# Two attention blocks on one core: the last twenty rounds with exponentials of 1024 columns, and the last head folded into the last group's projection

## The chip, the cores and the metric

The kernel runs on one core of a Trainium2 chip. The metric is the device time of one execution, in microseconds: 2844.2 us is the median of three runs (2843.77 to 2844.33).

## The reference

Two multi-head attention blocks A and B read the same x (2048 tokens, 512 features, 32 heads of 16), and a gate mixes their results:

```python
x = A_x
g = _sigmoid((x * gate_w).sum(-1, keepdims=True))
a = _A_ref(x, A_wqkv, A_wo)      # qkv = x @ wqkv; softmax(q k^T / 4) v per head; @ wo
b = _B_ref(x, B_wqkv, B_wo)
return g * a + (1 - g) * b
```

## The kernel before

After a prologue (the projections q, k, v) the kernel goes through 64 heads, 32 of block A and 32 of block B. A head has 16 tiles of 128 keys, and a **round** is one head and one tile of keys: 1024 rounds in all (`ROUNDS`). In a round, TensorE makes four score products of 128 keys by 512 queries (`score`, L594; product L602), ScalarE takes the exponential of each from PSUM (L604), and TensorE multiplies the exponentials with the values (`attend`, L555; product L563) into one PSUM bank `acc`. It has four column groups of 32 rows, one for each quarter of the queries; row 16 of a group is the sum of the exponentials, the softmax's denominator.

The scores carry the row's maximum as extra rows of q and k. The maxima of a head are made about a head ahead (`max_product`, L116), with a TensorE product of their own (L128) and a maximum on VectorE (L139). A loop over pairs of rounds writes each engine's order by hand: the string `FULL` puts score products (e), maximum products (m, A, B, x) and pieces of attend (digits, in quarters of a round) behind each other. Maxima are made for round r + 20 while round r is scored, so the last 20 rounds (1004 to 1023) have none; their order is the string `LATE = "ee2ee2ee2ee2"`. There, attend runs two rounds behind the scores.

When a head is done, ScalarE copies `acc` to `ev` (L580), which goes to DRAM (`od`). Eight heads are a group, and what is done for a group runs beside the rounds by a table (`at(round, function)`): `load_den` and `invert_den` bring the denominators and write their reciprocals to DRAM (`rd`); `load_num` brings numerators and reciprocals back (L409, L411), `normalize` multiplies them (L418), `split_out` splits the result into two fp32r parts (L423, L424), and `project_out` (L436) multiplies with wo in three products per tile of 128 tokens (L445), and VectorE adds to `o_acc` (L451).

The last group has seven heads that go this way; the 64th head goes another. It treats a quarter of the queries at a time: in its rounds the quarter's index is `kt // 4`, and the four column groups of `acc` hold four partial sums over keys. After each four rounds `acc` is copied (L571) and split (L574, L575). After the last round comes a list, `fill`: for each quarter, four `project_out` of the last group, `finish_den` (eight tiny products with `pick` that add the four denominators, L483, then reciprocal and gate, L485 and L486), and four `finish_out`, which project the last head's partial sums with wo's last 16 rows (three products, L496), add to `o_acc` (L497) and send the tile out (L499). Results there stand in five PSUM banks in turn (`result_bank`).

PSUM has eight banks: two of `ps_m1`, one double bank `ps_m2`, three of `ps_st`, and `acc`.

Of the kernel before, what the change touches and what calls it, by code (L numbers as in the profile page):

```python
# [51 lines left out]
def gated_mha(ctx: ExitStack, tc: tile.TileContext, xT, x, wqkv_a, wo_a, wqkv_b, wo_b, gate_w, out):  # L52
# [8 lines left out]
    ps_m1 = ctx.enter_context(tc.tile_pool(name="ps_m1", bufs=2, space=PSUM))  # L61
    ps_m2 = ctx.enter_context(tc.tile_pool(name="ps_m2", bufs=1, space=PSUM))
# [251 lines left out]
    ps_st = ctx.enter_context(tc.tile_pool(name="ps_st", bufs=3, space=PSUM))  # L314
    ps_acc = ctx.enter_context(tc.tile_pool(name="ps_acc", bufs=1, space=PSUM))
# [89 lines left out]
    def load_num(G, c):  # L405
        o, r, n = od[G], rd[G], gh[G] * DH
        num = work.tile([P, 512], F32, name="o_num", bufs=4)
        rb = work.tile([P, 512], F32, name="rb", bufs=4)
        nc.sync.dma_start(num[:n], bass.AP(tensor=o.tensor, offset=o.offset + c * 32 * 512,  # L409
                                           ap=[[NQ * 32 * 512, gh[G]], [512, DH], [1, 512]]))  # L410
        nc.sync.dma_start(rb[:n], bass.AP(tensor=r.tensor, offset=r.offset + c * 512,  # L411
                                          ap=[[S, gh[G]], [0, DH], [1, 512]]))
        nums[G, c] = num, rb

    def normalize(G, c):
        n = gh[G] * DH
        num, rb = nums[G, c]
        (dve if G == LAST else pool).tensor_tensor(num[:n], num[:n], rb[:n], op=ALU.mult)  # L418

    def split_out(G, c, slot):  # L420
        n = gh[G] * DH
        num, _ = nums.pop((G, c))
        pool.tensor_copy(ot[0][:n, slot], num[:n])  # L423
        (dve if G == LAST else pool).tensor_tensor(ot[1][:n, slot], num[:n], ot[0][:n, slot].bitcast(F32),  # L424
                                                   op=ALU.subtract)


    banks, fill_only = [], []

    def result_bank():  # L430
        banks.append(len(banks) % 5)
        if banks[-1] % 2 or not fill_only:
            return ps_m1.tile([P, 512], F32, name="ps_m1")
        return ps_st.tile([P, 512], F32, name="ps_st")

    def project_out(side, t):  # L436
        groups = SIDES[side]
        ps = result_bank()
        c, tt = divmod(t, 4)
        sl = slice(tt * P, (tt + 1) * P)  # L440
        for G in groups:
            n, g = gh[G] * DH, G % NG
            slot = c if G == LAST else g
            for i, (a, b) in enumerate(((0, 0), (1, 0), (0, 1))):
                pe.matmul(ps, ot[a][:n, slot, sl], wt[b][:n, g], start=G == groups[0] and i == 0,  # L445
                          stop=G == groups[-1] and i == 2)
        g = gate[min(side, 1)][:, t:t + 1]
        if side == 0:
            dve.tensor_scalar(o_acc[:, t], ps, g, None, op0=ALU.mult)
        else:  # L450
            dve.scalar_tensor_tensor(o_acc[:, t], ps, g, o_acc[:, t], op0=ALU.mult, op1=ALU.add)  # L451
# [6 lines left out]
    def load_tail():  # L458
        raw = work.tile([P, DM], F32, name="wo_raw", bufs=1)
        pool.memset(raw, 0.0)  # L460
        for c in range(NQ):
            nc.sync.dma_start(raw[32 * c:32 * c + DH], wo[1][DM - DH:DM, :])
        tail["raw"] = raw

    def split_tail():
        raw = tail["raw"]
        hi = core.tile([P, DM], F32R, name="wt_hi")
        lo = core.tile([P, DM], F32R, name="wt_lo")
        pool.tensor_copy(hi, raw)
        pool.tensor_tensor(lo, raw, hi.bitcast(F32), op=ALU.subtract)  # L470
        pick = core.tile([P, 2], F32R, name="pick")
        for i in range(2):
            with nc.allow_low_precision("sums of one 1 and three 0"):
                dve.tensor_reduce(pick[:, i:i + 1], ident[:, DH::32], op=ALU.add, axis=AX.X)
        tail["w"] = (hi, lo, pick)

    def finish_den(c):
        hi, lo = tail[c]
        pick = tail["w"][2]
# [4 lines left out]
        rg = small.tile([P, 4], F32, name="rg")  # L484
# [4 lines left out]
    def finish_out(t):  # L489
        c, tt = divmod(t, 4)  # L490
        hi, lo = tail[c]
        wh, wl, _ = tail["w"]
        ps = result_bank()
        sl = slice(tt * P, (tt + 1) * P)
# [4 lines left out]
        nc.sync.dma_start(out[t * P:(t + 1) * P, :], o_acc[:, t])  # L499
# [38 lines left out]
    fill = []  # L538
# [4 lines left out]
    for c in range(NQ):  # L543
# [4 lines left out]
    at(ROUNDS - 120, load_tail)  # L548
    at(ROUNDS - 100, split_tail)

# [4 lines left out]
    def attend(r, qa, qb):  # L555
        h, kt = divmod(r, NT)
        v, j = vg[h // HG], h % HG
        p = pt[r]
        final = h == NH - 1
        a = kt % 4  # L560
        first, last = (a == 0, a == 3) if final else (kt == 0, kt == NT - 1)
        for c in range(NQ):
            pe.matmul(acc[32 * c:32 * c + 17, qa * P:qb * P], v[:, 4 * a + c if final else kt, j],  # L563
                      p[:, c * 512 + qa * P:c * 512 + qb * P], start=first and qa == 0, stop=last,
                      tile_position=(0, 32 * c), skip_group_check=True)
        if qb < 4:
            return
        del pt[r]
        if final and last:
            ev = work.tile([P, 512], F32, name="ev")  # L570
            act.copy(ev, acc)  # L571
            hi = work.tile([P, 512], F32R, name="ev_hi")
            lo = work.tile([P, 512], F32R, name="ev_lo")
            pool.tensor_copy(hi, ev)  # L574
            pool.tensor_tensor(lo, ev, hi.bitcast(F32), op=ALU.subtract)  # L575
            tail[kt // 4] = (hi, lo)
        elif last:
            G, j = divmod(h, HG)
            ev = work.tile([P, 512], F32, name="ev")
            act.copy(ev, acc)  # L580
            nc.sync.dma_start(od[G][j].rearrange("c r t -> (c r) t"), ev)
# [12 lines left out]
    def score(r, c):  # L594
        h, kt = divmod(r, NT)
        if c == 0:
            pt[r] = ppool.tile([P, S], F32, name="p")
# [3 lines left out]
        ps = ps_st.tile([P, 512], F32, name="ps_st")  # L601
# [8 lines left out]
    LATE = "ee2ee2ee2ee2"  # L610
    after = {}

    for r in range(0, ROUNDS, 2):
        h, kt = divmod(r, NT)
        projects = []
        for rr in (r, r + 1):
            for fn, a in later.pop(rr, ()):
                if fn is project_out:
                    projects.append(a)
                else:  # L620
                    fn(*a)
        if kt == 0 and h + 2 < NH:
            load_stacks(h + 2)
        m = r + NT + LEAD
        scored = parts = 0
        waiting = len(halved)
        for step in FULL if m < ROUNDS else LATE:
            if step == "e":
                score(r + scored // 4, scored % 4)
                scored += 1  # L630
# [7 lines left out]
            else:  # L638
                for a in projects:
                    project_out(*a)  # L640
                projects = []
# [38 lines left out]
```

## Time and profile before

| | |
|---|---|
| median of three runs | 2844.2 us |
| the profiled execution's own time | 2844.78 us |
| its span in the profile | 2843.0 us |
| busy: TensorE, VectorE, ScalarE, GpSimd | 98%, 87%, 85%, 37% |
| the chain that ended last, by engine | TensorE 74%, VectorE 16%, ScalarE 8% |

The span is what the profiler saw between the first and the last instruction; the execution's own time is 1.78 us longer. TensorE's busy share counts matmuls that overlap in the array, so it is no measure of how full the array is. The stretch that the change touches is the end: rounds 1004 to 1023 and `fill`, from 2766 us to 2843 us.

### The profile page before, as it was taken

The numbers are of one execution on the slowest core, as the hardware profiler recorded it, in microseconds if no ns is written. First come the engines' busy times: TensorE is split into PE (matmuls) and PEld (weight loads), VectorE is DVE, ScalarE is ACT, GpSimd is POOL, SyncE is SP. The second block draws the span as 40 slices with busy tenths as digits, with TensorE's granted clock in tenths as the row PEclk, the third lists the DMA queues.
The fourth block names the chain that finished last, engine by engine and source line by source line (L and its number), as shares of the span: only waits on it lengthen the run. The fifth ranks groups of instructions, "written<-read, shape, count | busy, mean of one in ns | idle before, by whom it ended". The sixth has DMA issues, their size and how long they took to land.

```text
span 2843.0 us, 56787 instructions
## 1 busy us (share of the span) xinstructions
PE 2795.6 (98%) x22168; PEld 1230.1 (43%) x22168; DVE 2464.7 (87%) x3367; ACT 2412.5 (85%) x4696; POOL 1042.4 (37%) x1686
## 2 busy tenths in 40 slices
PE   8999999999999999999999999999999999999999
PEld 6877433333333333333333444433333333334445
DVE  3135899999999999999999988899999999998884
ACT  3221799999999999999999877899999999998785
POOL 1000355453433333333433555333333344345431
PEclk9999999999999999999999999999999999999999
DMA  6673333222332222232432342232222233233302
GB/s 237 203 229 122 82 69 78 58 52 54 66 58 55 55 43 58 52 56 54 85 54 52 92 94 62 54 56 51 60 43 56 54 70 70 54 72 80 76 6 91
DMA packets 83747, 214.30 MB, mean 75 GB/s; under 512 B 21878, under 2 KB 32086, under 8 KB 70934
## 3 DMA queue, kind: packets, MB, share of 16 engines
q1 hardware_dynamic: 80918, 201.76, 31.2%
q0 software_dynamic: 2560, 8.91, 1.3%
q8 instruction: 174, 2.85, 0.4%
q14 instruction: 95, 0.78, 0.1%
HBM read 145.87 MB, written 64.74 MB: 74 GB/s over the span
## 4 chain that ended last, share of the span: by engine, by line
PE 74%; DVE 16%; ACT 8%; issue 2%; DMA 0%; SPq 0%; ACTq 0%
PE acc L563 28%; PE ps_st L602 22%; DVE mxp L139 14%; PE ps_m L128 12%; PE ps_pro L228 6%; ACT p L604 5%; PE ps_m L445 3%; PE ps_pro L251 3%; ACT ev L580 1%; ACT fold L133 1%; DVE mxp L147 1%; DMA raw<-in_xT 0%; DVE mrow L157 0%; PE ps_st L445 0%; DVE rn L400 0%
## 5 line engine op out<-in xcount | busy, mean ns | idle before, releaser
L139 DVE TENSOR_REDUCE mxp<-ps_m 128x1 f32<-128x512 f32 (+1 forms) x2633 | 2190.3, 890 | 135.1 <-PE ps_m L128 61.0
L604 ACT ACTIVATE p<-ps_st 128x512 f32<-128x512 f32 x4096 | 2153.5, 610 | 177.0 <-PE ps_m L128 100.5
L128 PE MATMUL ps_m<-k_st,q_st 48*128 48x512 f32 x4096 | 1407.2, 441 | 5.3 <-DVE mxp L139 0.8
L602 PE MATMUL ps_st<-q_st,k_st 50*128 50x512 f32 x4096 | 1379.8, 438 | 0.0
L563 PE MATMUL acc<-p,vg 128*17 128x256 f32 (+1 forms) x12360 | 1182.8, 455 | 29.5 <-ACT ev L580 28.0
L602 PEld LDWEIGHTS ps_st<-q_st,k_st 50*128 50x128 f32 x4096 | 662.1, 184 | 801.6 <-ACT p L604 748.0
L128 PEld LDWEIGHTS ps_m<-k_st,q_st 48*128 48x128 f32 x4096 | 677.1, 184 | 251.8 <-DVE mxp L139 233.0
L134 POOL TENSOR_TENSOR fold<-fold 128x256 f32<-128x256 f32 x439 | 321.1, 731 | 1096.5 <-ACT fold L133 1096.5
L563 PEld LDWEIGHTS acc<-p,vg 128*17 128x17 f32 x12360 | 205.3, 95 | 466.3 <-issue 414.6
L136 POOL TENSOR_TENSOR fold<-fold 128x256 f32<-128x256 f32 x439 | 322.1, 734 | 36.6
L133 ACT COPY fold<-ps_m 128x512 f32<-128x512 f32 x439 | 261.3, 595 | 0.0
L135 POOL TENSOR_SCALAR fold<-fold 128x256 f32<-128x256 f32 x439 | 175.6, 400 | 38.5
L147 DVE TENSOR_REDUCE mxp<-fold 128x1 f32<-128x256 f32 x439 | 179.5, 409 | 0.0
L158 POOL CAST mparts<-mrow 128x16 fp32r<-128x16 f32 x64 | 12.6, 197 | 401.0 <-DVE mrow L157 401.0
L232 ACT CAST part<-ps_pro 128x1024 fp32r<-128x1024 f32 x32 | 32.5, 1015 | 132.9 <-PE ps_pro L228 132.9
L233 DVE TENSOR_TENSOR part<-ps_pro,part 128x1024 fp32r<-128x1024 f32 x32 | 39.2, 1225 | 111.4 <-ACT part L232 111.4
L445 PE MATMUL ps_m<-wo,ot 128*128 128x512 f32 (+1 forms) x354 | 90.9, 401 | 0.0
L254 ACT COPY v_st<-ps_pro 128x512 f32<-128x512 f32 x31 | 18.2, 587 | 77.4 <-PE ps_pro L251 77.4
L228 PE MATMUL ps_pro<-xh,whi 128*128 128x512 f32 x256 | 73.0, 404 | 8.8 <-ACT xh L214 8.7
L180 POOL DMA_DIRECT2D vg<-vd x32 | 25.6, 799 | 137.5 <-DMA vd<-v_st 137.1
L445 PEld LDWEIGHTS ps_m<-wo,ot 128*128 128x128 f32 (+1 forms) x354 | 63.9, 188 | 21.3 <-ACT fold L133 7.0
L228 PE MATMUL ps_pro<-xh,wlo 128*128 128x512 f32 x256 | 69.7, 395 | 0.0
(94 smaller groups left out, 822.1 us busy)
## 6 DMA issues: line engine op xcount, KB each, us to landing
k_st<-kd SPq DMA_DIRECT2D x128, 256.0 KB
q_st<-qd SPq DMA_DIRECT2D x128, 256.0 KB
qd<-part SPq DMA_DIRECT2D x32, 512.0 KB
kd<-part SPq DMA_DIRECT2D x32, 512.0 KB
k_st<-kd SPq DMA_DIRECT2D x128, 128.0 KB
q_st<-qd SPq DMA_DIRECT2D x128, 128.0 KB
od<-ev SPq DMA_DIRECT2D x63, 256.0 KB
vd<-v_st SPq DMA_DIRECT2D x32, 272.0 KB
```

Source lines behind the costliest of these rows:

```text
L128: pe.matmul(ps[:, o:o + 512], q[b:b + SC, t * P:(t + 1) * P], k[b:b + SC, c * 512:(c + 1) * 512], start=True, stop=True)
L133: act.copy(x, ps)
L134: pool.tensor_tensor(d, d, x[:, 256:], op=ALU.subtract)
L135: pool.tensor_scalar(d, d, 3.4028234e38, 0.0, op0=ALU.min, op1=ALU.max)
L136: pool.tensor_tensor(d, d, x[:, 256:], op=ALU.add)
L139: dve.tensor_reduce(mxp[h][:, t, part:part + 1], ps, op=ALU.max, axis=AX.X)
L147: dve.tensor_reduce(o, d, op=ALU.max, axis=AX.X)
L228: pe.matmul(ps[:, c * 512:(c + 1) * 512], a[:, k], b[:, k], start=n == 0, stop=n == 3 * KC - 1)
L445: pe.matmul(ps, ot[a][:n, slot, sl], wt[b][:n, g], start=G == groups[0] and i == 0, stop=G == groups[-1] and i == 2)
L563: pe.matmul(acc[32 * c:32 * c + 17, qa * P:qb * P], v[:, 4 * a + c if final else kt, j], p[:, c * 512 + qa * P:c * 512 + qb * P], start=fi ...
L602: pe.matmul(ps, k[b:b + SC + 2, kk * P:(kk + 1) * P], q[b:b + SC + 2, cc * 512:(cc + 1) * 512], start=True, stop=True)
L604: act.activation(pt[r][:, c * 512:(c + 1) * 512], ps, AF.Exp, scale=SCALE)
```

## The change

The rounds before 1004 keep their order. From round 1004 on:

- The pools `ps_m1`, `ps_m2` and `ps_st` are closed (`last_banks`), and in their place stand three double banks `ps_late` and one bank `ps_r`.
- `score_half` puts two score products into one double bank, and one exponential takes 1024 columns. Attend runs one round behind the scores, in pieces of a whole round.
- Copies of `acc` go to VectorE, all but the very last.
- The last head's partial sums are added on TensorE: `tail_sums(c)` multiplies both fp32r parts with a matrix `z` of ones and zeros. The result's rows 96 to 111 are the head's numerators, all its other rows the sum of its denominators. VectorE multiplies that onto the last group's normalized tile, in which rows 96 to 111 hold 1. The tile then holds eight heads scaled by the 64th's denominator, so that one projection serves all and the reciprocal with the gate ends it; `finish_out` is gone. `tail_sums` 0 to 2 run in rounds 1018, 1020 and 1022, the fourth in `fill`.
- In `load_num` of the last group, a GpSimd memset sets the rows that aren't loaded, and each load is two DMAs (6 heads and 1).

Cut to the core:

```diff
+    def last_banks():
+        early.close()
+        late["st"] = ctx.enter_context(tc.tile_pool(name="ps_late", bufs=3, space=PSUM))
+        late["r"] = ctx.enter_context(tc.tile_pool(name="ps_r", bufs=1, space=PSUM))
     def result_bank():
-        banks.append(len(banks) % 5)
-        if banks[-1] % 2 or not fill_only:
+        if not late:
             return ps_m1.tile([P, 512], F32, name="ps_m1")
-        return ps_st.tile([P, 512], F32, name="ps_st")
+        if not rest:
+            if scored[0] == 4 * ROUNDS:
+                for _ in range(3):
+                    two = late["st"].tile([P, 1024], F32, name="ps_late")
+                    rest.extend((two[:, :512], two[:, 512:]))
+            return late["r"].tile([P, 512], F32, name="ps_r")
+        return rest.pop(0)
...
+    def tail_sums(c):
+        z, pick = tail["ones"]
+        parts = tail[c]
+        ps = result_bank()
+        for i, a in enumerate(parts):
+            pe.matmul(ps, z, a, start=i == 0, stop=i == 1)
+        num, _ = nums[LAST, c]
+        dve.tensor_tensor(num, num, ps, op=ALU.mult)
+        split_out(LAST, c, c)
         ps = result_bank()
         for tt in range(4):
-            for i, a in enumerate((hi, lo)):
+            for i, a in enumerate(parts):
                 pe.matmul(ps[:, 2 * tt:2 * tt + 2], a[:, tt * P:(tt + 1) * P], pick, start=i == 0, stop=i == 1)
...
-        for i, (a, b) in enumerate(((hi, wh), (lo, wh), (hi, wl))):
-            pe.matmul(ps, a[:, sl], b, start=i == 0, stop=i == 2)
-        dve.scalar_tensor_tensor(o_acc[:, t], ps, tail["rg", c][:, tt:tt + 1], o_acc[:, t],
-                                 op0=ALU.mult, op1=ALU.add)
...
-        at(end + 4 + c // 2, load_num, LAST, c)
-        at(end + 10 + c // 2, normalize, LAST, c)
-        at(end + 11 + c // 2, split_out, LAST, c, c)
-    for c in range(NQ):
-        fill += [(project_out, 2, 4 * c + i) for i in range(4)]
-        fill.append((finish_den, c))
-        fill += [(finish_out, 4 * c + i) for i in range(4)]
+        at(end + 6 + 2 * (c // 2), load_num, LAST, c)
+        at(end + 10 + 2 * (c // 2), normalize, LAST, c)
+    for c in range(NQ - 1):
+        at(end + 10 + 2 * c, tail_sums, c)
+    fill = [(project_out, 2, t) for t in range(8)] + [(tail_sums, 3)]
+    fill += [(project_out, 2, t) for t in range(8, NT)]
...
+    def score_half(r, half):
+        if half == 0:
+            pt[r] = ppool.tile([P, S], F32, name="p")
+        ps = late["st"].tile([P, 1024], F32, name="ps_late")
+        for i in range(2):
+            score_product(r, 2 * half + i, ps[:, i * 512:(i + 1) * 512])
+            scored[0] += 1
+        act.activation(pt[r][:, half * 1024:(half + 1) * 1024], ps, AF.Exp, scale=SCALE)
...
+    last_banks()
+    for rr in range(scored[0] // 4, ROUNDS):
+        if rr % 2 == 0 and rr * 4 >= opened[0]:
+            open_rounds(rr)
+        for half in range(2):
+            score_half(rr, half)
+        while projects:
+            fn, *a = projects.pop(0)
+            fn(*a)
+        turn[0] = 0
+        attend_next(4 * rr - done[0])
+        while rows_due:
+            max_rows(rows_due.pop())
+    attend_next(4)
```

**Order, place 1.** TensorE where the pools change, in the program of the change (L617: score product, L572: attend, L129: maximum product; in brackets the engine on whose semaphore the instruction waits; numbers tell tiles apart):

```order
L617 MATMUL ps_st_35522<-q_st2_2010,k_st2_2011 128x512 [waits Activation_49]
L129 MATMUL ps_m2_35519<-k_st0_114,q_st0_113 128x512
L617 MATMUL ps_late_35542<-q_st2_2010,k_st2_2011 128x512 [waits DVE_49,Activation_49]
L617 MATMUL ps_late_35542<-q_st2_2010,k_st2_2011 128x512
L617 MATMUL ps_late_35546<-q_st2_2010,k_st2_2011 128x512 x2
L572 MATMUL acc_2015<-p_35468,vg_29644 17x512 x4
L572 MATMUL acc_2015<-p_35493,vg_29644 17x512 x4
L617 MATMUL ps_late_35564<-q_st2_2010,k_st2_2011 128x512 x2
```

Round 1004's first score product now waits for VectorE, for its last maximum, and two whole attends stand between round 1004's scores and round 1005's. Before, no product of the round waited for VectorE.

**Order, place 2.** TensorE in the last 20 rounds before (L602: score product, L563: attend):

```order
L602 MATMUL ps_st_35927<-q_st0_113,k_st0_114 128x512 [waits Activation_49]
L602 MATMUL ps_st_35930<-q_st0_113,k_st0_114 128x512 [waits Activation_49]
L563 MATMUL acc_2015<-p_35880,vg_29644 17x256 x4
L602 MATMUL ps_st_35937<-q_st0_113,k_st0_114 128x512 [waits Activation_49]
L602 MATMUL ps_st_35940<-q_st0_113,k_st0_114 128x512 [waits Activation_49]
L563 MATMUL acc_2015<-p_35880,vg_29644 17x256 x4
```

and in round 1018 of the change (L500: product with `z`, L507: product with `pick`):

```order
L617 MATMUL ps_late<-q_st_113,k_st_114 128x512 [waits PE_49]
L617 MATMUL ps_late<-q_st_113,k_st_114 128x512
L617 MATMUL ps_late<-q_st_113,k_st_114 128x512 [waits Activation_49]
L617 MATMUL ps_late<-q_st_113,k_st_114 128x512
L500 MATMUL ps_r<-ev_hi,z 128x512 [waits Pool_49]
L500 MATMUL ps_r<-ev_lo,z 128x512 [waits Pool_49]
L507 MATMUL ps_r<-pick,ev_hi 128x2 [waits DVE_49]
L507 MATMUL ps_r<-pick,ev_lo 128x2
```

Six more products with `pick` follow, then the attend. Both results stand in the one bank `ps_r`, so the products with `pick` wait for VectorE's multiplication, which reads the first.

**Order, place 3.** TensorE at the start of `fill`, before (each result is a tile of its own):

```order
L445 MATMUL ps_m1_36035<-wo0_2024,ot0_2026 128x512
L445 MATMUL ps_m1_36035<-wo0_2024,ot1_2027 128x512
L445 MATMUL ps_m1_36035<-wo1_2025,ot0_2026 128x512
L445 MATMUL ps_st_36040<-wo0_2024,ot0_2026 128x512
L445 MATMUL ps_st_36040<-wo0_2024,ot1_2027 128x512
L445 MATMUL ps_st_36040<-wo1_2025,ot0_2026 128x512
```

and in the change (L467: the projection's product; two results share a tile `ps_late`):

```order
L467 MATMUL ps_late_35937<-wo0_2024,ot0_2026 128x512
L467 MATMUL ps_late_35937<-wo0_2024,ot1_2027 128x512
L467 MATMUL ps_late_35937<-wo1_2025,ot0_2026 128x512
L467 MATMUL ps_late_35937<-wo0_2024,ot0_2026 128x512 [waits DVE_49]
L467 MATMUL ps_late_35937<-wo0_2024,ot1_2027 128x512
L467 MATMUL ps_late_35937<-wo1_2025,ot0_2026 128x512
L467 MATMUL ps_late_35938<-wo0_2024,ot0_2026 128x512 [waits PE_49]
```

The second product into a tile now waits for VectorE to have read the first result out of the other half of the tile.

## Rows read from the trace of the kernel before

**Rows 1.** Busy time by stretch: stretch, its length; busy us of PE, PEld, DVE, ACT, POOL; clock.
```profile
2770.00:2780.00 10.00, 9.63 (x90) 3.48 (x88) 0.00 (x0) 9.61 (x20) 0.00 (x0) 1.00 0.02 5
2800.00:2810.00 10.00, 9.53 (x90) 3.78 (x90) 4.54 (x6) 9.59 (x20) 3.11 (x5) 1.00 0.04 12
2820.00:2830.00 10.00, 10.00 (x53) 8.47 (x52) 9.47 (x16) 0.00 (x0) 3.82 (x4) 1.00 0.51 189
```

**Rows 2.** Timeline of ACT in the last rounds: start, us, what, xcount [idle before <-releaser].
```profile
2766.17 13.39 ACT L604 ACTIVATE p<-ps_st 128x512 f32<-128x512 f32 x25 [0.16 <-PE ps_st L602]
2779.45 0.59 ACT L580 COPY ev<-acc 128x512 f32<-128x512 f32 x1
2781.19 7.59 ACT L604 ACTIVATE p<-ps_st 128x512 f32<-128x512 f32 x14
2788.66 0.59 ACT L571 COPY ev<-acc 128x512 f32<-128x512 f32 x1
2807.52 4.52 ACT L604 ACTIVATE p<-ps_st 128x512 f32<-128x512 f32 x8
```

**Rows 3.** Groups by line and shape, ACT and DVE: busy us, mean ns | idle before.
```profile
L604 ACT ACTIVATE p<-ps_st 128x512 f32<-128x512 f32 x4096 | 2153.5, 610 | 177.0 <-PE ps_m L128 100.5 <-PE ps_st L602 53.0
L232 ACT CAST part<-ps_pro 128x1024 fp32r<-128x1024 f32 x32 | 32.5, 1015 | 132.9 <-PE ps_pro L228 132.9
L254 ACT COPY v_st<-ps_pro 128x512 f32<-128x512 f32 x31 | 18.2, 587 | 77.4 <-PE ps_pro L251 77.4
L418 DVE TENSOR_TENSOR o_num<-o_num,rb 112x512 f32<-112x512 f32 x4 | 2.7, 686 | 10.1 <-DMA rb<-rd 10.1
```

**Rows 4.** Timeline of the last rounds: last maximum, a score pair, last attend, copy of acc.
```profile
2766.74 1.22 DVE L139 TENSOR_REDUCE mxp<-ps_m 128x1 f32<-128x1024 f32 x1
...
2799.06 0.50 PE L602 MATMUL ps_st<-q_st,k_st 50*128 50x512 f32 x2
...
2799.49 0.63 PE L563 MATMUL acc<-p,vg 128*17 128x256 f32 x8
2799.60 7.57 ACT L604 ACTIVATE p<-ps_st 128x512 f32<-128x512 f32 x14 [0.15 <-PE ps_st L602]
...
2812.10 0.18 PEld L563 LDWEIGHTS acc<-p,vg 128*17 128x17 f32 x5 [0.26 <-ACT p L604]
...
2813.39 0.59 ACT L571 COPY ev<-acc 128x512 f32<-128x512 f32 x1 [1.35 <-PE acc L563]
```

**Rows 5.** Timeline of the fill: its first products, the products with pick, the last addition.
```profile
2813.12 0.53 PEld L445 LDWEIGHTS ps_st<-wo,ot 112*128 112x128 f32 x3 [0.85 <-issue]
...
2814.13 0.75 DVE L451 SCALAR_TENSOR_TENSOR o_acc<-ps_st,gate,o_acc 128x512 f32<-128x512 f32 x1 [8.00 <-PE ps_st L445]
...
2814.82 0.75 DVE L451 SCALAR_TENSOR_TENSOR o_acc<-ps_m,gate,o_acc 128x512 f32<-128x512 f32 x1
...
2815.78 0.19 PEld L483 LDWEIGHTS ps_m<-pick,ev_hi 128*128 128x128 f32 x1
...
2816.79 0.19 PEld L496 LDWEIGHTS ps_st<-wt_hi,ev_hi 128*128 128x128 f32 x1
...
2839.28 0.75 DVE L497 SCALAR_TENSOR_TENSOR o_acc<-ps_st,rg,o_acc 128x512 f32<-128x512 f32 x1
```

**Rows 6.** Busy time by stretch, columns as rows 1, around the two falls of the clock.
```profile
19.00:22.40 3.40, 1.84 (x8) 1.17 (x8) 2.29 (x2) 3.09 (x4) 0.00 (x0) 1.00 0.10 31
22.40:25.80 3.40, 3.40 (x10) 2.63 (x9) 1.90 (x3) 0.98 (x2) 0.00 (x0) 0.50 0.58 233
295.50:298.90 3.40, 2.63 (x13) 1.40 (x12) 2.57 (x4) 2.25 (x5) 2.98 (x2) 1.00 0.41 140
298.90:305.70 6.80, 6.46 (x25) 2.44 (x27) 5.11 (x7) 4.20 (x8) 2.48 (x4) 0.50 1.08 193
```

**Rows 7.** Timeline of PE in the prologue: four products at either level of the clock.
```profile
13.72 1.07 PE L228 MATMUL ps_pro<-xh,wlo 128*128 128x512 f32 x4
...
23.21 1.91 PE L228 MATMUL ps_pro<-xl,whi 128*128 128x512 f32 x4
```

More of the change, by code (lines that the diff above doesn't have):

```diff
@@ L428, in gated_mha @@
-    banks, fill_only = [], []
+        final = (G, c) == (LAST, NQ - 1)
+        if final:
+            act.copy(ot[0][:, slot], num)
+        else:
+            pool.tensor_copy(ot[0][:, slot], num)
+        (dve if G == LAST and not final else pool).tensor_tensor(
+            ot[1][:, slot], num, ot[0][:, slot].bitcast(F32), op=ALU.subtract)
+    late, rest = {}, []
+    def last_banks():
+        early.close()
+        late["st"] = ctx.enter_context(tc.tile_pool(name="ps_late", bufs=3, space=PSUM))
+        late["r"] = ctx.enter_context(tc.tile_pool(name="ps_r", bufs=1, space=PSUM))
@@ L471, in split_tail, with tail_ones @@
+            return
+        g = gate[1][:, t:t + 1] if side == 1 else tail["rg", c][:, tt:tt + 1]
+        dve.scalar_tensor_tensor(o_acc[:, t], ps, g, o_acc[:, t], op0=ALU.mult, op1=ALU.add)
+        if side == 2:
+            nc.sync.dma_start(out[t * P:(t + 1) * P, :], o_acc[:, t])
+    tail = {}
+    def tail_ones():
+        z = core.tile([P, P], F32R, name="z")
         pick = core.tile([P, 2], F32R, name="pick")
-        for i in range(2):
-            with nc.allow_low_precision("sums of one 1 and three 0"):
+        groups = ident.rearrange("p (c e) -> p e c", c=NQ)
+        with nc.allow_low_precision("sums of one 1 and three 0"):
+            dve.tensor_reduce(z[:, 96:112], groups[:, :DH], op=ALU.add, axis=AX.X)
+            for i in range(2):
@@ L474, in split_tail @@
                 dve.tensor_reduce(pick[:, i:i + 1], ident[:, DH::32], op=ALU.add, axis=AX.X)
[L475 to L479, printed above, removed]
+        for o in (z[:, :96], z[:, 112:]):
+            dve.tensor_copy(o, pick[:, :1].bitcast(F32).to_broadcast(list(o.shape)))
+        tail["ones"] = z, pick
+    def tail_sums(c):
[7 more added lines that the diff above has]
+        split_out(LAST, c, c)
@@ L570, in attend @@
             ev = work.tile([P, 512], F32, name="ev")
-            act.copy(ev, acc)
+            if kt == NT - 1:
+                act.copy(ev, acc)
+            else:
+                dve.tensor_copy(ev, acc)
             hi = work.tile([P, 512], F32R, name="ev_hi")
             lo = work.tile([P, 512], F32R, name="ev_lo")
-            pool.tensor_copy(hi, ev)
+            if kt == NT - 1:
+                act.copy(hi, ev)
+            else:
+                pool.tensor_copy(hi, ev)
             pool.tensor_tensor(lo, ev, hi.bitcast(F32), op=ALU.subtract)
@@ L579, in attend @@
             ev = work.tile([P, 512], F32, name="ev")
-            act.copy(ev, acc)
+            if late:
+                dve.tensor_copy(ev, acc)
+            else:
+                act.copy(ev, acc)
             nc.sync.dma_start(od[G][j].rearrange("c r t -> (c r) t"), ev)
@@ L592, in attend_next, with score_product @@
             n -= qb - qa
-    def score(r, c):
+    def score_product(r, c, ps):
         h, kt = divmod(r, NT)
-        if c == 0:
-            pt[r] = ppool.tile([P, S], F32, name="p")
         q, k = q_st[h % 3], k_st[h % 3]
@@ L623, in gated_mha @@
             load_stacks(h + 2)
+    for r in range(0, ROUNDS - NT - LEAD, 2):
+        open_rounds(r)
         m = r + NT + LEAD
-        scored = parts = 0
+        n = parts = 0
         waiting = len(halved)
-        for step in FULL if m < ROUNDS else LATE:
+        for step in FULL:
             if step == "e":
-                score(r + scored // 4, scored % 4)
-                scored += 1
+                score(r + n // 4, n % 4)
+                n += 1
             elif step in "mABx":
```

106 lines of the change are left out of this document (47 added, 59 removed).

## The prediction

> **What bounds the kernel now.** First the busy time by stretch, for the end alone, since the change leaves everything before round 1004 as it is. In the last rounds ScalarE is busy 9.6 us of 10, VectorE hardly at all [rows 1]; in the fill TensorE is busy all the time, VectorE nearly so, ScalarE not. So the rounds hang on exponentials and the fill on products.
>
> Next ScalarE's timeline [rows 2]. 25 exponentials run without a gap in 13.39 us: one each (13.39 - 0.61) / 24 = 0.53 us; 14 in 7.59 us give 0.54; I take 0.535. The first of the 25 belongs to round 1003, so the 80 of the last 20 rounds start at 2766.17 + 0.53 = 2766.70 and end at 2807.52 + 4.52 = 2812.04. 80 x 0.535 = 42.8 of these 45.3 us; the other 2.5 us are four copies of `acc` on ScalarE, 0.63 each with their gaps. Then the fill, from 2813.12 to the span's end at 2843.0: 29.9 us [rows 5].
>
> **Part by part.**
>
> *Exponentials of 1024 columns: 4.3 us less.* No exponential of this width is in the trace. From PSUM, ScalarE takes 587 ns for 512 columns and 1015 ns for 1024 [rows 3]: 428 ns per 512 more. One wide exponential then follows the last after 0.535 + 0.428 = 0.963 us, in place of 1.07: 0.107 us less, 40 times. Bounds: 0, if width saves nothing; 2 x 0.428 = 0.856 each, if all the fixed part is hidden, 8.6 us. I take 4.3, since the wide cast shows its fixed part once. [...]
>
> *Copies of `acc` on VectorE: 2.5 us less on ScalarE.* VectorE takes between 0.686 us (its cheapest pass over 512 columns here [rows 3]) and 0.75 [rows 5]. It is covered: attend's result is there 1.29 us after its first weights (2812.10 to 2813.39 [rows 4]), so 0.06 + 1.29 + 0.72 = 2.07 us after the exponential that attend waited for, when the next one (1.93 us a round) has just ended; TensorE's slack below takes the 0.14. Without that slack, 0.14 x 4 = 0.6 us.
>
> *The pools change: 2.6 us more.* Round 1004's first product waits until VectorE's last maximum ends, 2766.74 + 1.22 = 2767.96 [rows 4]; from a score pair to its exponential are 0.54 us (2799.06 to 2799.60), so ScalarE goes on at 2768.55 instead of 2766.70: 1.85 us. Behind the scores stand two whole attends of 1.02 us (2812.10 to 2813.12 [rows 4, 5]); round 1005's scores come 0.66 + 2.04 us after round 1004's, and ScalarE, done in 1.93, waits 0.7 us more.
>
> *A plain round.* On TensorE: two score pairs, 0.43 to the attend behind a pair (2799.06 to 2799.49) and 0.23 for the other, and 1.0 for the attend: 1.66 us, under ScalarE's 1.93. ScalarE stays the bound.
>
> *Three `tail_sums` in the rounds: 6.0 us more.* From the first weights of the `z` products to VectorE's start: a group of three takes 1.01 (2813.12 to 2814.13 [rows 5]), two take 0.78. VectorE's multiplication out of PSUM 0.72; back to TensorE 0.06 (2812.04 to 2812.10); eight `pick` products 1.01 (2815.78 to 2816.79): 2.57 us in TensorE's queue, the attend and the next scores behind them. Two rounds with a sum take TensorE 2 x 1.66 + 2.57 = 5.9 us, ScalarE's exponentials 3.9: 2.0 lost three times. The three score buffers only cover the first wait in part. Bounds: 0, if the buffers cover all; 7.7, if nothing overlaps.
>
> *The loads before them: nothing.* The last group's reciprocals must be there by round 1018. They come by 16 DMAs on SP in place of 8, half of them behind memsets on GpSimd. Before, `normalize` waited for them 10.1 us in all with nobody behind it [rows 3]; now TensorE's sums stand behind it. Between head 62's copy, in round 1008, and round 1018 are 9 rounds, 17 us, which I take as cover; without it a DMA's couple of microseconds, 0 to 2, are in the range.
>
> *The fill: 5.1 us less.* Before: 16 x 6 products and four times eight small ones, TensorE without a gap. Now 16 x 3. But every second result waits for VectorE to read the one before it. With product 1.01 after a wait [rows 5], the next result 0.69 later (2814.13 to 2814.82), addition 0.75, back 0.06, a pair of tiles takes 1.01 + 0.69 + 0.75 + 0.06 = 2.51 us, not 1.4. First two tiles done at 2.45; three pairs to 10.0; the last `tail_sums`: 0.72, 0.06, 1.01 to 11.8; the next tile 1.76 to 13.55; two pairs, one tile (0.69), one pair: 21.8. The span ended 2.97 us after the last addition's end, 2839.28 + 0.75 [rows 5]: 24.8 us against 29.9.
>
> *The constants `z`: 0.3 us more* on a VectorE that is busy in round 924 (0 to 0.5).
>
> *Sum:* -4.3 - 2.5 + 2.6 + 6.0 - 5.1 + 0.3 = -3.0 us against the profiled execution's 2844.78: 2841.8. That execution lies 0.6 over the median, so 2841.2 in these terms.
>
> **The clock.** [...] So I expect falls: one for each sum, two in the fill. Four products take 1.91 us at the lower level against 1.07 [rows 7], about 0.2 us more each. A fill pair then takes 2.51 + 1.2 = 3.7 us; two rounds with a sum 5.9 + 2 x 0.85 (attend doubled, an estimate) + 6 x 0.2 = 8.8. A fall of 3.4 us loses 3.4 x (1 - 2.51 / 3.7) = 1.1 us in either place. Five: 5.5 us. Forecast: 2841.2 + 5.5 = **2846.7 us**.
>
> [...]
>
> **Rivals.** What a measurement of this kernel can tell from no change is about 0.2%, 5.7 us: below 2838.5 or above 2849.9.
> - *The clock holds.* For it: after 305.7 us TensorE was stopped now and then through a thousand rounds, and no stretch read at the end shows less than full clock [rows 1]. Against: none of those stops comes as often as the fill's. 2841.2.
> - *Slower: the clock stays low* from the first sum to the end. It decides if the low level outlasts the busy stretch behind each stop. Against: both falls ended. Sums 3 x 2.9, six pairs 7.2, four single tiles 2.4: 2841.2 + 18.3 = 2859.5.
> - *Slower: width saves nothing* (two narrow ones' price): 2846.7 + 4.3 = 2851.0. The wide cast speaks against it.
> - *Faster: the sums are hidden* by the buffered scores: 6.0 and three falls less, 2837.4, or 2835.2 without any fall. Against: TensorE's order puts the next scores behind the wait.
> - That the sum on TensorE or the wide exponential isn't issued can be excluded by the order of the instructions.
>
> **Numbers.** Forecast 0.50 (2843 to 2851), clock holds 0.20, stays low 0.12, no gain by width 0.06, sums hidden 0.12. Range 2838 to 2856: it leaves out most of the hidden sums and of the low clock. Faster: 0.09 of the hidden sums and 0.05 of the held clock, 0.14. Slower: 0.12, 0.05, and 0.09 of the forecast, 0.26. Same: 0.60.
>
> **What would show it.** Exponentials of 1024 columns about 1.03 us long, starting 0.96 apart; ScalarE idle before round 1004 and by about 2 us behind each of the three sums; copies of `acc` on VectorE with no wait of ScalarE; in the fill VectorE's additions in pairs, 2.5 us a pair; about 24 to 27 us from the first L467 to the end; stretches of clock 0.50 after 2795 us. Wrong would be: exponentials without a gap across round 1019, additions every 0.75 us in the fill, or clock 1.00 to the end.

## The result: 2849.2 us against 2844.2, and the profile after

| | before | after |
|---|---|---|
| median (16 runs each) | 2844.2 us | 2849.2 us |
| lowest to highest | 2842.9 to 2847.5 | 2843.4 to 2854.0 |
| span of the profiled execution | 2843.0 us | 2849.7 us |
| its mean granted clock | 0.998 | 0.992 |

The ratio is 1.0016, its interval 1.0009 to 1.0024: a slowdown of about 5 us. After's runs scatter over 11 us, and their time goes with their mean clock: the five at 0.992 to 0.994 have a median of 2851.7 us, the five at 0.996 of 2847.3, the one at 0.998 took 2843.4. The profiled execution (own time 2851.5 us) lies 2.3 us over the median, so what follows shows one of its longer executions.

ScalarE's timeline after, which answers to [rows 2]: start, us, what, xcount [idle before <-releaser].

```profile
2764.83 0.60 ACT L625 ACTIVATE p<-ps_st 128x512 f32<-128x512 f32 x1 [0.16 <-PE ps_st L617]
2767.36 1.94 ACT L634 ACTIVATE p<-ps_late 128x1024 f32<-128x1024 f32 x2 [1.93 <-PE ps_late L617]
2769.81 25.77 ACT L634 ACTIVATE p<-ps_late 128x1024 f32<-128x1024 f32 x28 [0.52 <-PE ps_late L617]
2800.45 1.94 ACT L634 ACTIVATE p<-ps_late 128x1024 f32<-128x1024 f32 x2 [4.86 <-PE ps_late L617]
2803.43 1.94 ACT L634 ACTIVATE p<-ps_late 128x1024 f32<-128x1024 f32 x2 [1.05 <-PE ps_late L617]
2810.21 1.94 ACT L634 ACTIVATE p<-ps_late 128x1024 f32<-128x1024 f32 x2 [4.84 <-PE ps_late L617]
2813.20 1.94 ACT L634 ACTIVATE p<-ps_late 128x1024 f32<-128x1024 f32 x2 [1.05 <-PE ps_late L617]
2817.91 1.94 ACT L634 ACTIVATE p<-ps_late 128x1024 f32<-128x1024 f32 x2 [2.77 <-PE ps_late L617]
```

Two wide exponentials take 1.94 us and 28 take 25.77, so one follows the other after (25.77 - 1.94) / 26 = 0.917 us and lasts 1.02. At the pools' change ScalarE waits 1.93 + 0.52 us. Then come 15 rounds nearly without a gap, and in the last five rounds ScalarE stands 4.86 + 1.05 + 4.84 + 1.05 + 2.77 = 14.6 us. From the last narrow exponential to the last of all it is 2765.43 to 2819.85, 54.4 us; before 45.3.

Busy time by stretch after, with the columns of [rows 1]: the rounds before the first sum, the stretch behind it, and the fill.

```profile
2767.36:2795.58 28.22, 26.60 (x180) 7.51 (x178) 4.84 (x9) 27.70 (x30) 7.99 (x13) 1.00 0.19 61
2796.20:2813.30 17.10, 16.32 (x67) 6.38 (x66) 4.84 (x10) 5.91 (x7) 2.86 (x4) 0.51 0.08 29
2820.87:2849.70 28.83, 19.00 (x62) 12.45 (x58) 13.13 (x19) 1.83 (x3) 2.55 (x2) 0.72 0.38 146
```

The clock is at its lower level for 17.1 us from the first sum on (0.51), again in 2816.7 to 2820.1 (0.53), and from 2833.8 to the end (0.50). Two timelines of the changed kernel follow, first TensorE's, then VectorE's: each at the first sum, then in the fill at full clock, and last in the fill at the lower one.

```profile
2793.62 0.50 PE L500 MATMUL ps_r<-ev_hi,z 128*128 128x512 f32 x1
...
2795.93 0.35 PE L507 MATMUL ps_r<-pick,ev_hi 128*128 128x2 f32 x1 [1.59 <-DVE o_num L502]
...
2797.71 1.91 PE L572 MATMUL acc<-p,vg 128*17 128x512 f32 x8
2799.55 1.22 PE L617 MATMUL ps_late<-q_st,k_st 50*128 50x512 f32 x4
...
2823.37 1.64 PE L467 MATMUL ps_late<-wo,ot 128*128 128x512 f32 x6 [0.84 <-DVE o_acc L473]
...
2842.96 2.93 PE L467 MATMUL ps_late<-wo,ot 128*128 128x512 f32 x6 [0.84 <-DVE o_acc L473]
```

```profile
2794.59 0.69 DVE L427 TENSOR_TENSOR o_num<-o_num,rb 128x512 f32<-128x512 f32 x1 [2.07 <-DMA rb<-rd]
2795.20 0.68 DVE L502 TENSOR_TENSOR o_num<-o_num,ps_r 128x512 f32<-128x512 f32 x1
...
2824.37 1.43 DVE L473 SCALAR_TENSOR_TENSOR o_acc<-ps_late,rg,o_acc 128x512 f32<-128x512 f32 x2 [1.05 <-PE ps_late L467]
2826.85 1.44 DVE L473 SCALAR_TENSOR_TENSOR o_acc<-ps_late,rg,o_acc 128x512 f32<-128x512 f32 x2 [1.05 <-PE ps_late L467]
...
2842.16 0.75 DVE L473 SCALAR_TENSOR_TENSOR o_acc<-ps_late,rg,o_acc 128x512 f32<-128x512 f32 x1 [0.53 <-PE ps_late L467]
2844.65 0.75 DVE L473 SCALAR_TENSOR_TENSOR o_acc<-ps_late,rg,o_acc 128x512 f32<-128x512 f32 x1 [1.74 <-PE ps_late L467]
2845.93 0.75 DVE L473 SCALAR_TENSOR_TENSOR o_acc<-ps_late,rg,o_acc 128x512 f32<-128x512 f32 x1 [0.53 <-PE ps_late L467]
```

The products with `pick` wait 1.59 us, because VectorE's multiplication comes behind a normalization (the second quarter's) that waits for its load. Then each of them, the attend (1.91 us against 1.05) and the scores (1.22 against 0.73) run at the lower clock, and the next scores come 5.9 us after the last. In the fill TensorE stands 0.84 us for VectorE in each pair of tiles, and a pair of additions comes every 2.48 us at full clock and every 3.77 at the lower one (2842.16 to 2845.93). The fill takes 28.8 us; before, 29.9.

### The profile page after: what moved, and what is told of

Read it like the earlier page. It is cut to its first block, busy times and chain, and to the rows that moved or that the text cites. A ratio compares the mean times of both kernels' runs of the same rounds, so it can differ in the third digit from the quotient of the medians.

```text
span 2849.7 us, 56375 instructions
## 1 busy us (share of the span) xinstructions
PE 2794.1 (98%) x21968; PEld 1221.0 (43%) x21968; DVE 2458.8 (86%) x3361; ACT 2408.1 (85%) x4654; POOL 1046.6 (37%) x1690
## 4 chain that ended last, share of the span: by engine, by line
PE 73%; DVE 17%; ACT 7%; issue 2%; DMA 1%; POOL 0%; SPq 0%; ACTq 0%; DVEq 0%
PE acc L572 27%; PE ps_st L617 21%; DVE mxp L140 15%; PE ps_m L129 12%; PE ps_pro L229 6%; ACT p L625 5%; PE ps_pro L252 3%; PE ps_m L467 3%; ACT ev L598 1%; ACT fold L134 1%; DVE mxp L148 1%; DMA raw<-in_xT 0%; PE ps_late L467 0%; PE ps_late L617 0%; DVE mrow L158 0%
## 5 line engine op out<-in xcount | busy, mean ns | idle before, releaser
L625 ACT ACTIVATE p<-ps_st 128x512 f32<-128x512 f32 x4016 | 2111.5, 610 | 174.9 <-PE ps_m L129 110.6
L129 PE MATMUL ps_m<-k_st,q_st 48*128 48x512 f32 x4096 | 1406.9, 441 | 5.4 <-DVE mxp L140 0.8
L617 PE MATMUL ps_st<-q_st,k_st 50*128 50x512 f32 x4016 | 1356.1, 437 | 0.0
L572 PE MATMUL acc<-p,vg 128*17 128x256 f32 (+1 forms) x12200 | 1184.9, 460 | 28.2 <-ACT ev L598 27.6
L617 PEld LDWEIGHTS ps_st<-q_st,k_st 50*128 50x128 f32 x4016 | 650.9, 184 | 784.4 <-ACT p L625 740.3
L129 PEld LDWEIGHTS ps_m<-k_st,q_st 48*128 48x128 f32 x4096 | 677.3, 184 | 252.1 <-DVE mxp L140 233.7
L572 PEld LDWEIGHTS acc<-p,vg 128*17 128x17 f32 x12200 | 203.7, 95 | 464.1 <-issue 412.3
L467 PE MATMUL ps_m<-wo,ot 128*128 128x512 f32 x336 | 85.6, 401 | 0.0
L229 PE MATMUL ps_pro<-xl,whi 128*128 128x512 f32 x256 | 69.4, 393 | 0.0
```

The source lines that it names most:

```text
L129: pe.matmul(ps[:, o:o + 512], q[b:b + SC, t * P:(t + 1) * P], k[b:b + SC, c * 512:(c + 1) * 512], start=True, stop=True)
L229: pe.matmul(ps[:, c * 512:(c + 1) * 512], a[:, k], b[:, k], start=n == 0, stop=n == 3 * KC - 1)
L467: pe.matmul(ps, ot[a][:, slot, sl], wt[b][:, g], start=G == groups[0] and i == 0, stop=G == groups[-1] and i == 2)
```

## Experiments

Ratios are to the kernel before, measured on the same chip. Its median lay between 2844.0 and 2844.6 us each time, so the medians of different versions are compared as they are. What is read from a timeline holds for the one execution profiled. A *fall* is a stretch in which the granted clock is at its lower level, 0.50.

**A bank for each result of the fill.**

```diff
-                    rest.extend((two[:, :512], two[:, 512:]))
+                    rest.append(two[:, :512])
```

> The rounds stay as in the change; in the fill each result has a tile of its own, so that no product waits for VectorE to read its neighbour. In the changed kernel's profile the stretch from the first projection product to the end took 28.8 us. Theory (the shared tile makes the waits, the waits make the clock fall): additions every 0.70 us, 16 of them 11.2 us, the last sum's multiplication and small steps 1.4, first product 1.0, last output 3.0: 17 to 19 us, clock at full level in the fill, median 2838 to 2841. Rival 1 (the clock is low in the fill whatever the waits are, carried over from the rounds): 16 tiles of 1.28 us behind one another and the sum, 25 to 27 us, median 2846 to 2848. Rival 2 (VectorE, not the tile, sets the pairs): nothing changes, median 2847 to 2851.

Measured: 2838.5 us, ratio 0.9978 (0.9968 to 0.9987). The fill by busy time, and VectorE's timeline of three additions in it:

```profile
2820.04:2836.50 16.46, 12.60 (x60) 10.20 (x58) 11.92 (x19) 1.83 (x3) 2.59 (x2) 0.95 0.66 256
```

```profile
2821.75 2.13 DVE L473 SCALAR_TENSOR_TENSOR o_acc<-ps_late,rg,o_acc 128x512 f32<-128x512 f32 x3
```

Additions follow at 0.69 us, the fill takes 16.5 us, and the clock is at full level in it but for the last 1.7 us, behind TensorE's last product. The theory holds: one line is worth 10.7 us of the medians. Both rivals fall.

The rounds of this version are the change's own. ScalarE's timeline behind the three sums:

```profile
2801.54 1.94 ACT L634 ACTIVATE p<-ps_late 128x1024 f32<-128x1024 f32 x2 [2.82 <-PE ps_late L617]
2804.45 1.94 ACT L634 ACTIVATE p<-ps_late 128x1024 f32<-128x1024 f32 x2 [0.96 <-PE ps_late L617]
2809.28 1.94 ACT L634 ACTIVATE p<-ps_late 128x1024 f32<-128x1024 f32 x2 [2.90 <-PE ps_late L617]
2811.78 1.94 ACT L634 ACTIVATE p<-ps_late 128x1024 f32<-128x1024 f32 x2 [0.56 <-PE ps_late L617]
2817.08 1.94 ACT L634 ACTIVATE p<-ps_late 128x1024 f32<-128x1024 f32 x2 [3.35 <-PE ps_late L617]
```

Here the same three stops of TensorE (1.20, 0.78 and 0.78 us; in the change's profile 1.59, 0.78 and 0.78) cost 10.6 us and not 14.6: the clock fell three times for 3.4 us (from 2800.7, 2807.5 and 2814.4), once for each sum, and rose each time.

**Products with `z` and `pick` in different rounds.** `tail_sums` is split in two, the second part one round later.

```diff
+        plan.setdefault(end + 10 + 2 * c, []).append((sum_z, c))
+        plan.setdefault(end + 11 + 2 * c, []).append((sum_pick, c))
```

> The fill stays as in the change; the eight products with the pick matrix come one round after the products with z, so that TensorE doesn't stand for VectorE's multiplication. In the changed kernel's profile ScalarE stood idle for 14.6 us in all behind the three sums (4.86, 1.05, 4.84, 1.05, 2.77). Theory (the wait makes the clock fall, and the low clock is most of those 14.6 us): clock at full level through the rounds, idle 3 to 5 us in all for the 1.65 us of products per sum, median 2838 to 2842. Rival (the products themselves, not the wait, cost the time): three waits of 0.8 us go, 2.4 us, the clock falls as before, median 2845 to 2848.

Measured: 2843.7 us, ratio 0.9999 (0.9989 to 1.0008); 5.5 us under the change. ScalarE's idle times behind the sums are 0.28, 0.69, 0.37, 3.85 and 1.77 us, 7.0 in all: half of the 14.6 goes, where the theory expected two thirds or more, and the median lies between the theory's range and the rival's. The 3.85 have a cause that neither theory had. VectorE's timeline there:

```profile
2807.48 0.69 DVE L427 TENSOR_TENSOR o_num<-o_num,rb 128x512 f32<-128x512 f32 x1 [2.00 <-DMA rb<-rd]
2808.09 0.68 DVE L501 TENSOR_TENSOR o_num<-o_num,ps_r 128x512 f32<-128x512 f32 x1
2809.48 0.69 DVE L436 TENSOR_TENSOR ot<-o_num,ot 128x512 fp32r<-128x512 f32 x1 [0.71 <-POOL ot L435]
2810.09 0.68 DVE L591 COPY ev<-acc 128x512 f32<-128x512 f32 x1
```

A load holds up the normalization, and in VectorE's queue the multiplication and the copy of `acc` stand behind it. TensorE waits for both (0.91 us for the multiplication, 0.87 for the copy), and the clock falls from 2809.9 to 2816.7 (0.52).

**No sums in the rounds.**

```diff
-        at(end + 10 + 2 * c, tail_sums, c)
+        at(end + 10 + 2 * c, no_sums, c)
```

> Leaves out the first three sums: neither products with z and pick nor multiplication and reciprocal for these quarters; loads, normalization, splitting and the fill are as in the change. It gives the whole price of the three sums in the rounds. Theory: exponentials of 1024 columns 0.917 us apart without a gap from round 1005 to 1023, clock at full level until the fill, 14.6 us less in the rounds than in the changed kernel's profile and 11 to 13 less in the median: 2836 to 2839; the fill still takes 25 to 29 us. Rival (the clock falls in these rounds without any sum, since attend and scores alone leave TensorE idle too often): stretches of the lower clock before the fill, ScalarE idle by about 1 us a round there, median over 2842.

Measured: 2843.3 us (2839.4 to 2847.9), ratio 0.9995 (0.9986 to 1.0004): the theory falls, since the sums are not the only stop. The timelines of TensorE and of VectorE in round 1019:

```profile
2804.31 1.91 PE L576 MATMUL acc<-p,vg 128*17 128x512 f32 x8 [4.33 <-DVE ev L587]
```

```profile
2802.36 0.69 DVE L427 TENSOR_TENSOR o_num<-o_num,rb 128x512 f32<-128x512 f32 x1 [2.57 <-DMA rb<-rd]
2802.97 0.68 DVE L436 TENSOR_TENSOR ot<-o_num,ot 128x512 fp32r<-128x512 f32 x1
2803.57 0.68 DVE L587 COPY ev<-acc 128x512 f32<-128x512 f32 x1
```

The copy of `acc` waits here as well, and the attend that begins the next quarter waits 4.33 us for it. The first and the last of the 16 loads on SP:

```profile
2784.02 0.76 SPq L419 DMA_DIRECT2D o_num<-od  x1
...
2796.49 0.55 SPq L421 DMA_DIRECT2D rb<-rd  x1
```

The last is issued 12.5 us after the first (before, 8 in 6.1, 2786.21 to 2792.31): SP waits 2.3 us for GpSimd's memsets and issues twice as many. In the change itself the loads take as long (2783.17 to 2795.63), but the sums delay the rounds, and that hides a part of it. The rival's rule (the clock falls without a stop) is not borne out: the one fall in these rounds, from 2803.9 to 2810.7, begins at the end of the 4.33 us in which TensorE stood. The median all the same lies in the rival's range; only the next version, without this stop, parts the two.

**The same with memsets and six heads' numerators loaded 12 rounds earlier.**

```diff
+        at(end - 6 + 2 * (c // 2), early_num, c)
         at(end + 6 + 2 * (c // 2), load_num, LAST, c)
```

> Leaves out the first three sums, as the version without sums did (2843.27 us, with a stop of TensorE of 4.33 us in round 1019 for a copy of acc that stood on VectorE behind a normalization that waited for its load); and here the memsets and the loads of six of the last group's seven heads come 12 rounds earlier. Theory (the late loads are the rest of the loss in the rounds): exponentials without a gap from round 1005 to the end, the clock at full level until the fill, median 2835 to 2839. Rival (the stop has another cause, or the clock falls in these rounds anyway): 2841 to 2844.

Measured: 2835.4 us, ratio 0.9965 (0.9953 to 0.9977); 7.9 us less than without the earlier loads. ScalarE's timeline:

```profile
2773.97 35.19 ACT L655 ACTIVATE p<-ps_late 128x1024 f32<-128x1024 f32 x38 [2.71 <-PE ps_late L638]
```

The last 38 exponentials come without a gap, and the granted clock over them is 0.99. Here the wait at the pools' change brought a fall of its own (clock 0.51 from 2768.0 to 2775.0; 2.71 us before round 1005 in place of 0.52).

**The change with these earlier loads alone.** The edit is the same, on the change itself.

> The change with nothing but the earlier memsets and loads; sums and fill as in the change (2849.2 us). Theory (the late loads make the first sum's wait longer and start the long fall of the clock): that wait 0.8 us in place of 1.6, shorter falls, 1 to 5 us less: 2844 to 2848. Rival (the sums' own waits are enough for the falls): 2848 to 2851.

Measured: 2846.5 us, ratio 1.0006 (0.9996 to 1.0016): 2.7 us less than the change, as the theory had it, though the intervals of the two ratios overlap. The first sum's wait is 0.84 us. The clock still falls for 3.4 and 13.7 us in the rounds, so the sums' own waits are enough for long falls: in that the rival was right.

**TensorE kept busy in its waits.** The waits of the sums and of the fill stay; four products into a tile that nobody reads stand in front of each.

```diff
+        for _ in range(4):
+            pe.matmul(spare[0][:, :512], z, tail[0][0], start=True, stop=True)
```

> Adds work: in each wait of TensorE (three sums and the fill's waits) four products of 512 columns into a tile that nothing reads, 0.86 us at full clock for a wait of 0.84; all waits and their order stay. Theory (the stops let the clock fall, and the falls cost more than the stops): clock at full level to the end; rounds with 2 us idle of ScalarE behind each sum, the fill 25 to 27 us; median 2838 to 2843, in spite of the added work. Rival 1 (the time goes into the waits themselves): clock or not, nothing gained, 2848 to 2852. Rival 2 (the clock falls anyway, so the added products take 1.7 us each time at the lower level): slower, 2852 to 2858.

Measured: 2842.8 us, ratio 0.9996 (0.9986 to 1.0006); 6.4 us under the change, with more work (in the fill four of the added products take 1.01 us, 2818.13 to 2819.14, not 0.86). Busy time from the first sum to the end, and ScalarE's timeline behind the three sums:

```profile
2797.00:2841.10 44.10, 39.06 (x202) 22.84 (x201) 20.41 (x35) 12.59 (x15) 6.29 (x7) 1.00 0.31 113
```

```profile
2801.00 3.77 ACT L647 ACTIVATE p<-ps_late 128x1024 f32<-128x1024 f32 x4 [2.76 <-PE ps_late L630]
2807.45 3.81 ACT L647 ACTIVATE p<-ps_late 128x1024 f32<-128x1024 f32 x4 [2.67 <-PE ps_late L630]
2813.68 1.94 ACT L647 ACTIVATE p<-ps_late 128x1024 f32<-128x1024 f32 x2 [2.43 <-PE ps_late L630]
```

The clock stays at full level, ScalarE loses 7.9 us at the sums in place of 14.6, and the fill takes 24.5 us (2816.64 to 2841.10; 25 to 27 expected) in place of 28.8. Both rivals fall: the order and its waits are as before, a pair in the fill still takes 2.50 us, and it is the clock that differs.

**All of it together:** banks for the fill, sums in rounds of their own (the third quarter's in the fill, its splitting on ScalarE and GpSimd), earlier loads, and the attend of round 1002 ahead of the pools' change. Three versions change one thing of it.

```diff
+    attend_next(4 * scored[0] // 4 - 4 - done[0])
     last_banks()
...
+    for r, fn, c in ((8, sum_pick, 0), (10, sum_z, 0), (12, sum_pick, 1), (13, sum_z, 1)):
+        plan.setdefault(end + r, []).append((fn, c))
...
+    for i, step in ((8, (sum_pick, 3)), (6, (sum_z, 3)), (4, (sum_pick, 2)), (2, (sum_z, 2))):
+        fill.insert(i, step)
```

> The change with every wait taken out that the first runs showed: a tile for each result in the fill; products with pick and with z in rounds of their own (1016, 1018, 1020, 1021), the third quarter's sum in the fill; the memsets and the loads of the last group's first six heads issued 12 rounds earlier, so that normalization on VectorE no longer holds up the copies of acc; the attend of round 1002 ahead of the pools' change. Theory (waits and the clock falls behind them are the whole loss; the wide exponentials are worth 0.917 us each): ScalarE idle 2.0 to 2.5 us at the pools' change and under 2 us after it, 40 x 0.917 = 36.7 us of rounds, a fill of 19 to 20 us bound by TensorE's products, the clock at full level: median 2826 to 2831. Rival (TensorE's clock falls in these rounds and in the fill also without stops): 2833 to 2841.

> As the version with every wait taken out, but with two exponentials of 512 columns in place of each of 1024. It prices the width where ScalarE is the bound. Theory by the changed kernel's profile (0.917 us against 2 x 0.535): 0.153 x 40 = 6.1 us more than with wide ones. The prediction's own figure: 0.107 x 40 = 4.3 us more. Rival (TensorE is the bound at 1.83 us a round anyway): 0 to 2 us more.

> As the version with every wait taken out, but the attends of rounds 1002 and 1003 both stay behind the scores of round 1004, as in the change. Theory: ScalarE idle 1.9 us before round 1004 and 0.5 us before 1005, or 1.8 us where the clock falls behind the wait for VectorE's last maximum: 0.5 to 1.8 us more than the version with every wait taken out. Rival (the score buffers cover it): no difference.

> As the version with every wait taken out, but ScalarE copies acc, as before the change (four copies in the rounds). Theory: ScalarE is the bound of the rounds, so 4 x 0.63 = 2.5 us more. Rival (TensorE's queue or VectorE's handover was the bound at those four places, and a copy on an idle ScalarE comes sooner): 0 to 1 us more, or less time.

| version | median | ratio to before | first late exponential to the end of the last |
|---|---|---|---|
| all | 2828.8 | 0.9947 (0.9934 to 0.9959) | 2773.36 to 2812.41, 39.0 us |
| narrow exponentials | 2830.2 | 0.9948 (0.9935 to 0.9960) | 2768.70 to 2809.51, 40.8 |
| attends behind the scores | 2829.6 | 0.9945 (0.9932 to 0.9959) | 2767.92 to 2808.97, 41.0 |
| copies on ScalarE | 2829.6 | 0.9948 (0.9935 to 0.9960) | 2772.62 to 2812.64, 40.0 |

The version with all of it beats both kernels, 15.2 us under before. In its profile ScalarE is idle 1.94 us at the pools' change and 1.83 us behind it and the clock stays at full level to TensorE's last product (1.00 over the rounds, 0.98 over the fill, whose last product ends at 2827.4), as expected; the fill takes 17.9 us, less than the 19 to 20. The four medians can't be told apart; the stretch of the rounds, which the length of earlier falls doesn't touch, can only be compared for one execution each. There the width is worth 1.8 us, not 6.1; the copies 1.0, not 2.5; the attend's place 2.0, with a fall of the clock in it. ScalarE's timeline in the narrow version shows why the width is worth so little:

```profile
2768.70 25.59 ACT L656 ACTIVATE p<-ps_late 128x512 f32<-128x512 f32 x52 [1.92 <-PE ps_late L638]
```

One narrow exponential follows the other after (25.59 - 0.6) / 51 = 0.49 us, not 0.535. The rival's figure, 0 to 2 us, came true, but not its reason: ScalarE has no gap here, so it is the bound.

**Narrow exponentials, a bank for each.** The pool has six single tiles in place of three double ones.

```diff
-        ps = late["st"].tile([P, 1024], F32, name="ps_late")
+            ps = late["st"].tile([P, 512], F32, name="ps_late")
```

> As the version with every wait taken out with two narrow exponentials, but each score product has a bank of its own (six single banks in place of three double ones), so that each narrow exponential has a handover of its own from TensorE. With a shared double bank they came 0.490 us apart, in the kernel before 0.535. Theory 1 (the handover per tile sets 0.535): 0.53 to 0.54 us apart, 80 x 0.045 = 3.6 us longer than with the double bank, 2832 to 2834. Theory 2 (0.535 was the pace of TensorE's order in the kernel before, with attend in halves): 0.49 us apart, 2829 to 2831.

Measured: 2829.7 us, ratio 0.9948 (0.9933 to 0.9963). Busy time by stretch here, then in the kernel before in the same rounds:

```profile
2768.15:2793.70 25.55, 25.31 (x164) 7.67 (x164) 2.96 (x8) 25.55 (x52) 4.03 (x7) 1.00 0.17 56
```

```profile
2766.70:2779.40 12.70, 12.70 (x120) 4.76 (x112) 1.67 (x4) 12.21 (x25) 0.42 (x2) 1.00 0.02 5
```

Theory 2: 0.49 us apart, ScalarE busy for all of 25.55 us. In the kernel before it was idle for 0.49 us of 12.70, in gaps too short for the timeline to show (one of 0.1 us in each round), and an exponential behind a gap doesn't overlap with the one before: the 0.535 held a wait for TensorE. Six single banks and an attend in whole rounds take it away with narrow exponentials too; which of the two does it was not tried.

## Why the prediction was right or wrong

The forecast, 2846.7, was 2.5 us under the median, inside its range, and the class (no change to tell at 0.2%) holds narrowly. Its mechanism, waits of TensorE and falls of its clock that eat the gain, is what the runs show: with the waits taken out the kernel is 15.2 us faster than before, and with the waits kept and the clock held it is 6.4 us faster than the change.

That the number came so near is in part luck. In the profiled executions the rounds take 9.1 us more (forecast 5.1, three falls among them) and the fill 1.1 less (forecast 2.9, with two falls); 1.3 us are won back ahead of the rounds, which is no more than the scatter there. And the time hangs on how long the falls last, the prologue's too: 2843.4 to 2854.0 us in 16 runs. The sizes, by the prediction's own terms:

- **Wide exponentials, -4.3.** The step 0.428 per 512 columns holds (0.49 + 0.428 = 0.918, measured 0.917). The base was wrong: 0.535 was taken for ScalarE's own pace, though the row before it, 9.6 us busy of 10 [rows 1], showed the gap. Against before, 40 x (1.07 - 0.917) = 6.1 us became available; the part of the width in it is 40 x (0.98 - 0.917) = 2.5, the rest comes with the banks and the order. A wide exponential's record is 1.02 us long, but the next one starts 0.917 us after it; back to back, a pair of narrow ones takes 0.98, so 63 ns a pair are what the width saves.
- **Copies of `acc`, -2.5 and covered.** Gone from ScalarE, but not covered: they inherit VectorE's queue. Behind a normalization that waits for a load, a copy made TensorE wait (4.33 us without the sums, 0.87 with the sums apart).
- **Pools, +2.6.** 1.93 + 0.52 = 2.45 us. (The forecast's 1.85 us are 1.80 by its own rows: 2767.96 + 0.54 is 2768.50.) That the clock can fall at this wait, too, was missed: in five of the eight profiled executions that keep this order ScalarE waits 1.65 to 2.71 us before round 1005, in place of 0.52.
- **Sums, +6.0.** 14.6 us in the profiled execution, 10.6 in another with the same rounds. With TensorE kept busy, at full clock, 7.9 remain, the added products and the waits for the late loads among them. The rest is the clock.
- **Loads, 0.** This step failed. Its 17 us of cover were counted from copy to sum (2776.56 to 2793.62 in the change), but 6.6 of them pass before the first load is issued (2783.17), and SP's queue of 16 loads behind memsets takes 12.5 more, until 2795.63. The couple of microseconds allowed for one DMA was too short as well: the last load of the second quarter is issued at 2790.30, and the normalization that waits for it starts at 2794.59, 4.3 us later. Earlier loads are worth 2.7 us in the change and 7.9 without the sums.
- **Fill, -5.1 to 24.8 us.** At full clock, with the unread products, 24.5 us: right, pair by pair (2.48 us, said 2.51). The waits by tile are what it costs: with a bank for each result it is 16.5.
- **Constants `z`, +0.3.** Not visible: the last narrow exponential ended at 2765.4 us, against 2766.8 before, when the prologue had one fall more (3.4 us). The change's profile has one fall of 6.8 us in the prologue, from 297.7. In the profiles of the change and eight of its versions that last exponential ended between 2765.4 and 2767.2, in three others between 2770.7 and 2771.4; one of these is the version with all of it, whose mean clock is 0.997, although it lost nothing in the rounds (1.00) and little in the fill (0.98).
- **Clock, +5.5 for five falls of 3.4 us.** One fall for each sum and two in the fill was the author's estimate, which no run shows; the profiled execution has three, one across the first two sums, one behind the third and one in the fill. The place was right, the length not: 17.1 us, 3.4, and 15.9 to the end. In the fill it cost about 28.8 - 24.5 = 4.3 us, in the rounds 14.6 - 7.9 = 6.7. The version with a bank for each result had falls in its rounds as forecast, three of 3.4 us: about (10.6 - 7.9) / 3 = 0.9 us each, said 1.1. So the price of a fall was about right, and what was missed is that a fall can last five times as long. In the fill of the change a pair takes 2.48 us at one clock and 3.77 at the other. The rival "clock stays low" thus came true for part of the end, and the longer falls are offset in part by the exponentials' larger gain (1.8 us more).

What stays open: why the same stop ends in a long fall in one execution and in a short one in another (17.1 us against 3.4; 2843 to 2854 us in the runs, the prologue's falls among the causes), and the exact worth of width and copies, which the timed runs can't tell from no change.

## What to carry to other kernels

When an addition puts a wait into TensorE's queue, price the wait twice: its own length (here 0.84 us a pair in the fill), and the work that runs at the lower clock behind it (a pair in 3.77 us, not 2.48); four products that nobody reads in the gap tell the two apart (a fill of 24.5 us, not 28.8), and a second bank takes both away (16.5 us). A bank shared by two results, or a queue shared by an urgent copy and an operation that waits for a load, costs more here than the instruction that it saves: 10.7 us for the bank, a stop of 4.33 us for the queue, in which the copy itself took 0.68. Before an engine's pace is taken as its own, look for small gaps in its busy share: the 4% that were missing here were a wait.

## What the hardware showed that was not expected

- TensorE stayed at the lower clock for 17.1 us in which it was busy 16.32; the falls of the prologue, also busy nearly throughout, ended after 3.4 and 6.8 us [rows 6]. The work was of another kind here, scores and attends, not projections, but that alone is not the reason: with the same rounds three falls ended after 3.4 us in the version with a bank for each result.
- Forty products that nobody reads, 0.2 us and more each, made the changed kernel 6.4 us faster.
- The length of a ScalarE record is not its price: narrow exponentials, 0.60 us long in the kernel before, have a mean of 0.81 us in the version with single banks, and there they come 0.49 us apart (the group's row in 2771 to 2790 us; busy us, mean ns | idle before).

```profile
L654 ACT ACTIVATE p<-ps_late 128x512 f32<-128x512 f32 x41 | 20.2, 808 | 0.0
```
